# Second layer of a fused attention and feed-forward kernel on Trainium2: seven half-size products in place of eight, for all token chunks but the first

## The chip, the cores and the metric

The kernel runs on one core of one Trainium2 chip. The metric is the device time of one execution in microseconds (us). Matrix products run on TensorE (PE), which reads SBUF and writes PSUM. ScalarE (ACT), VectorE (DVE) and GpSimd (POOL) do elementwise work; SyncE (SP) here only starts DMAs. Every engine works through its own queue in order and waits for others by semaphores.

## The reference

Attention over 8 batches, 8 heads and 576 positions, with 16 extra "beacon" keys and values in front that every query sees, then two linear layers with a leaky ReLU between them on the 4608 tokens:

```python
def _attn_ref(q, k, v, beacon_k, beacon_v):
    k_all = np.concatenate([beacon_k, k], axis=2)
    v_all = np.concatenate([beacon_v, v], axis=2)
    scores = scale * np.matmul(q, k_all.transpose(0, 1, 3, 2))
    scores = np.where(causal, -1000000000.0, scores)
    a = np.exp(scores - scores.max(-1, keepdims=True))
    a /= a.sum(-1, keepdims=True) + 1e-09
    return np.matmul(a, v_all)

def _moe_ref(x, w_in, w_out):          # x: 4608 x 512, w_in: 512 x 2048, w_out: 2048 x 512
    h = x @ w_in
    g = np.maximum(0.01 * h, h)
    return g @ w_out
```

## The kernel before

**Attention.** A group is one batch and a pair of heads; there are 32 groups, four to a batch. Groups 0 to 7 are a hand-written head, a string of short codes that `run` expands. From group 8 on, the work is a list of events sorted by a due time in units of one group: loads of q and k (`load_natural`, issued by POOL), their transposes by DMA (`turn_pair`, issued by SP), a block of three score tiles (`block`: matmuls, then exponentials on ACT, then masks on POOL), the value matmuls in two halves (`value`: matmuls, then a reciprocal and a multiplication on DVE), and `x_turn`, two or three DMA transposes issued by SP that write the group's result into `xT`, which holds the tokens as columns.

**The two layers.** Tokens are taken in nine chunks of 512. One `up` (`moe1`) makes one 128 x 512 piece of layer 1: four matmuls of 512 columns into one PSUM bank, and a leaky ReLU on ACT into the bf16 tile `gT`; 16 of them make a chunk. One `down` (`moe2`) is a quarter of a 128-token output tile of layer 2: four matmuls of 512 columns, accumulated over 16 pieces of `gT` in one bank; 16 downs make a chunk. After the fourth quarter DVE copies the bank to `osb` (two buffers) and SP stores it. The very last tile is split into 384 and 128 columns, the second part copied and stored by ACT.

**Order.** The program order of all five queues is that of the Python program. Between events, `fill` places ups and downs so that they spread evenly over a batch: `aim` is the share of the units due. `ready` is the number of chunks whose tokens are finished; a batch makes one more ready, the last batch two. `finish` of a batch's last group also holds back three downs (`KEPT`) to be run before the first up of the new chunk. An up may be one chunk ahead of the downs (`gT` has two buffers); where both kinds can go, they take turns. So in a middle batch three old downs are followed by 16 ups and then 13 downs of the same chunk. I call the passage from the last up to the first down "the turn". After the last attention work, chunks 7 and 8 are left: 16 ups, then ups of chunk 8 and downs of chunk 7 by turns, then the downs of chunk 8 alone.

**PSUM.** Four single banks (`ps_one`, tag "one") are shared by the accumulators of ups, downs, values, transposes and the first score tile of each block; four more, in pairs, serve the other score tiles.

Of the kernel before, what the change touches and what calls it, by code (L numbers as in the profile page):

```python
# [8 lines left out]
FP32 = mybir.dt.float32  # L9
BF16 = mybir.dt.bfloat16  # L10
# [5 lines left out]
def kernel(  # L16
# [42 lines left out]
    QT = [(0, 112), (112, 128), (240, 128), (368, 128), (496, 80)]  # L59
    NA, NK = 4, 8  # L60
    LAID = 2 * NPAIR
    TURNED = 8
# [13 lines left out]
    singles = ctx.enter_context(tc.tile_pool(name="singles", bufs=1))  # L76
    qkpool = ctx.enter_context(tc.tile_pool(name="qkpool", bufs=2))
    natpool = ctx.enter_context(tc.tile_pool(name="natpool", bufs=6))
    headpool = ctx.enter_context(tc.tile_pool(name="headpool", bufs=2))
    gpool = ctx.enter_context(tc.tile_pool(name="gpool", bufs=2))  # L80
    opool = ctx.enter_context(tc.tile_pool(name="opool", bufs=2))
    ps_sc = ctx.enter_context(tc.tile_pool(name="ps_sc", bufs=2, space=bass.MemoryType.PSUM))
# [8 lines left out]
    w_out_sb = singles.tile([128, NF, DM], BF16, name="w_out_sb")  # L91
    w_out_r = moe_w_out.rearrange("(c p e) d -> p c (e d)", p=128, e=2)

    def w_in_cols(fc, j):
        at = fc % 8 // 2 * 256 + fc % 2
        return w_in_sb[fc // 8][:, j, at : at + 255 : 2]

    xT = singles.tile([128, NJ, NTOK], BF16, name="xT")
    bkT = singles.tile([128, B, NPAIR, NB], BF16, name="bkT")
# [3 lines left out]
    k_bufs = [k_all[:, i] for i in range(NK)]  # L103
    first_k = singles.tile([RP, 2, RI, D], FP32, name="first_k")
    k_nat0 = singles.tile([RP, RI, 2, D], BF16, name="k_nat0")
# [30 lines left out]
    def raw_of(b, grp):  # L136
        if (b, grp) not in qk_raw:
            qk_raw[b, grp] = (
                qkpool.tile([128, 2, RI, D], BF16, name="q_raw"),
                qkpool.tile([128, 2, RI, D], BF16, name="k_raw"),  # L140
            )
        return qk_raw[b, grp]
# [13 lines left out]
    def load_first_keys():  # L156
        nc.sync.dma_start(out=first_k, in_=k[0, 0:2].rearrange("h (p i) d -> p h i d", i=RI))

# [207 lines left out]
    def value(g, half):  # L366
# [19 lines left out]
        )  # L386

    def x_transposes(g, copy):
        b, hp = divmod(g, NPAIR)
        x_nat, _ = xs.pop(g)  # L390
        ps = ps_one.tile([128, 1024], BF16, name="tp", tag="one")
        for t, (q0, rows) in enumerate(QT):
            nc.tensor.transpose(
                ps[:, q0 : q0 + rows],
                x_nat[0:rows, t].rearrange("p e d -> p (e d)"),
                ident[0:rows, 0:rows],
            )
        copy(out=xT[:, hp, b * S : (b + 1) * S], in_=ps[:, 0:S])

    def x_turn(g):  # L400
        b, hp = divmod(g, NPAIR)
        x_nat, _ = xs.pop(g)
        t1 = NKB if b < B - 1 else NKB - 1
        dst = xT[:, hp, b * S : b * S + 112 + (t1 - 1) * 128]
        nc.sync.dma_start_transpose(
            out=dst[:, 112:].rearrange("c (t r) -> c t r", r=128),
            in_=x_nat[:, 1:t1].rearrange("r t e d -> r (t e d)"),
        )
        if t1 < NKB:
            nc.sync.dma_start_transpose(  # L410
                out=xT[:, hp, NTOK - 80 :], in_=x_nat[0:80, t1].rearrange("r e d -> r (e d)")
            )
        nc.sync.dma_start_transpose(  # L413
            out=dst[:, 0:112], in_=x_nat[0:112, 0].rearrange("r e d -> r (e d)")
        )
# [3 lines left out]
    def moe1(i, fc):  # L419
        if i not in gT:  # L420
            gT[i] = gpool.tile([128, NF, 512], BF16, name="gT")
        acc = ps_one.tile([128, 512], FP32, name="acc", tag="one")
        for j in range(NJ):
            nc.tensor.matmul(  # L424
                out=acc,
                lhsT=w_in_cols(fc, j),
                rhs=xT[:, j, i * 512 : (i + 1) * 512],
                start=(j == 0),
                stop=(j == NJ - 1),
            )  # L430
        nc.scalar.activation(out=gT[i][:, fc, :], in_=acc, func=AF.Prelu, alpha=0.01)  # L431

    early = {}

    def moe1_early(n, j):
        if j == 0:
            early[n] = ps_sc.tile([128, 2, 512], FP32, name="sc", tag="sc")
            if 0 not in gT:
                gT[0] = gpool.tile([128, NF, 512], BF16, name="gT")
        for e in range(2):  # L440
            fc = 2 * n + e
            nc.tensor.matmul(
                out=early[n][:, e],
                lhsT=w_in_cols(fc, j),
                rhs=xT[:, j, 0:512],
                start=(j == 0),
                stop=(j == NJ - 1),
            )
        if j == NJ - 1:
            nc.scalar.activation(  # L450
                out=gT[0][:, 2 * n : 2 * n + 2, :], in_=early[n], func=AF.Prelu, alpha=0.01
            )
            done1[0] += 2

    acc2 = [None]

    def moe2(i, t, quarter):
        t0 = i * 512 + t * 128
        if t0 + 128 < NTOK:
            moe2_part(i, t, quarter, quarter + 1, 0, DM, nc.vector.tensor_copy, nc.sync)  # L460
            return
        n = 3 * DM // 4
        if quarter < 3:
            moe2_part(i, t, 4 * quarter // 3, 4 * (quarter + 1) // 3, 0, n, nc.vector.tensor_copy, nc.sync)
        else:
            moe2_part(i, t, 0, 4, n, DM, nc.scalar.copy, nc.scalar)

    def moe2_part(i, t, q0, q1, lo, hi, copy, eng):
        if q0 == 0:
            acc2[0] = ps_one.tile([128, 512], FP32, name="acc", tag="one")  # L470
        acc = acc2[0][:, 0 : hi - lo]
        for fc in range(q0 * 4, q1 * 4):
            nc.tensor.matmul(  # L473
                out=acc,
                lhsT=gT[i][:, fc, t * 128 : (t + 1) * 128],
                rhs=w_out_sb[:, fc, lo:hi],
                start=(fc == 0),
                stop=(fc == NF - 1),
            )
        if q1 < 4:  # L480
            return
        t0 = i * 512 + t * 128
        osb = opool.tile([128, hi - lo], FP32, name="osb" if lo == 0 and hi == DM else f"osb{lo}")
        copy(out=osb, in_=acc)  # L484
        eng.dma_start(out=out[t0 : t0 + 128, lo:hi], in_=osb)

    done1, done2, ready, turn, first_down, held = [0], [0], [0], [0], [0], [0]

    def fill():
        i1, fc = divmod(done1[0], NF)  # L490
        i2, n2 = divmod(done2[0], NF)
        can1 = i1 < ready[0] and (i1 < 2 or i2 > i1 - 2)
        can2 = i2 < NCH and i2 < i1 and done1[0] >= first_down[0]
        if held[0] and can2:
            held[0] -= 1
            down()
        elif can1 and (turn[0] == 0 or not can2):
            up()
        elif can2:
            down()  # L500
        return can1 or can2

    def up():
        i1, fc = divmod(done1[0], NF)
        assert i1 < ready[0]
        moe1(i1, fc)
        done1[0] += 1
        turn[0] = 1

    def down():  # L510
        i2, n2 = divmod(done2[0], NF)
        moe2(i2, n2 // 4, n2 % 4)
        done2[0] += 1
        turn[0] = 0

# [39 lines left out]
    def run(steps):  # L555
        for step in steps.split():
# [25 lines left out]
            elif op == "u":  # L582
                up()
            elif op == "P":
                moe1_early(*a)
            elif op == "d":
                down()
            elif op == "w":
                unused(*a)
            elif op == "W":  # L590
                unused_ahead(*a)
            elif op == "i":
                load_w_in(a[0])
            elif op == "o":
                load_w_out(a[0])
            else:
                raise ValueError(step)
# [11 lines left out]
    with order:  # L609
# [12 lines left out]
        unused(13)  # L622
        nc.scalar.copy(out=k_nat0[:, :, 0], in_=first_k[:, 0])
        nc.vector.tensor_copy(out=k_nat0[:, :, 1], in_=first_k[:, 1])
        run("q0.1 k0 w2.384 s0.0 m0.0 w3.256 s0.1 q1 s0.2 m0.1 k1 s0.3 m0.2")
# [6 lines left out]
        beacon_transposes(2, B)  # L632
        run("m7.1 m7.2 N9.1 u b8.2 b9.2 b10.2 b11.2 x6 v7.0 T9 v7.1 d d d N10.0 N10.1 d V2.0 V2.1 x7 T10")

# [21 lines left out]
        def has_down():  # L656
            return done2[0] // NF < done1[0] // NF

# [27 lines left out]
        for at, _, what, args in events:  # L686
            while w + 2 < len(ends) and at > ends[w + 1]:
                w, d0 = w + 1, done1[0] + done2[0]
            todo = 2 * NF * ready[0] - KEPT - d0
            aim = d0 + todo * (at - ends[w]) / (ends[w + 1] - ends[w])  # L690
# [7 lines left out]
            what(*args)  # L698
        while done2[0] < NCH * NF:
            fill()  # L700
# [30 lines left out]
```

The softmax here doesn't subtract the row's maximum and nothing guards it: scores larger than these inputs give would overflow.

## Time and profile before

| | |
|---|---|
| runs shown | 338.26, 337.88, 338.02 us; median 338.02 us |
| profiled execution | span 339.9 us |
| PE busy | 328.5 us (97%), 2950 matmuls |
| ACT, POOL, DVE busy | 187.1, 180.8, 82.8 us |
| layer 1 matmuls (L424) | 553 recorded (576 in the program), 135.9 us |
| layer 2 matmuls (L473) | 568 recorded (592 in the program), 131.6 us |
| end of the last matmul | about 336.8 us |

The profiled execution lasted about 1.9 us longer than the median of the runs; its own span is the base for sums. Busy times of PE overlap, since matmuls are pipelined: a 512-column matmul is shown with 380 ns, while one follows another after about 216 ns. "x" is a count; "idle before" is the time an engine stood still before a group, with what ended it.

### The profile page before, as it was taken

Reading aid. Unit: us, or ns where it says so; the run is one execution under the profiler, and the core shown is the slowest. Engines: PE = TensorE matmul, PEld = TensorE weight load, DVE = VectorE, ACT = ScalarE, POOL = GpSimd, SP = SyncE. Lnnn points to the kernel's source line nnn. Section 1 sums busy time; section 2 is a strip of 40 time slices with the busy share of each in tenths; the row PEclk is TensorE's granted clock in tenths of the full one; section 3 lists DMA queues with packets and bytes.
Section 4 is the critical chain, followed back from the end, with each engine's and each line's share of the span. In section 5 each row is a group of like instructions: output and inputs, shape, how many; then the busy total and the mean of one; then the engine's idle time right before and its main releaser. Section 6 shows DMA issues by size and latency. Waiting matters only on the chain.

```text
span 339.9 us, 7458 instructions
## 1 busy us (share of the span) xinstructions
PE 328.5 (97%) x2950; PEld 170.7 (50%) x2997; DVE 82.8 (24%) x202; ACT 187.1 (55%) x312; POOL 180.8 (53%) x354
## 2 busy tenths in 40 slices
PE   8989999999996999999999999999999999999996
PEld 5574565455553455544554555545455544444443
DVE  3572354021222112311330232212321220000111
ACT  4969761778554583478536843685368205633300
POOL 8894969968987475668656966675221000000000
PEclk9999999999998999999999999999999999999999
DMA  8999999999999999999999999999211130000012
GB/s 135 129 194 169 149 212 129 177 181 122 163 154 186 160 113 139 137 123 103 110 183 137 112 114 159 159 117 123 89 56 39 23 110 33 0 31 33 31 63 91
DMA packets 151922, 39.84 MB, mean 117 GB/s; under 512 B 143008, under 2 KB 145184, under 8 KB 151888
## 3 DMA queue, kind: packets, MB, share of 16 engines
q0 software_dynamic: 99824, 18.54, 83.0%
q1 hardware_dynamic: 51648, 20.70, 34.0%
q8 instruction: 23, 0.38, 0.5%
q10 hardware_dynamic: 416, 0.13, 0.2%
q14 instruction: 11, 0.09, 0.1%
HBM read 37.22 MB, written 9.44 MB: 137 GB/s over the span
## 4 chain that ended last, share of the span: by engine, by line
PE 82%; DMA 11%; POOL 3%; issue 2%; SPq 0%; DVE 0%; ACT 0%; POOLq 0%; DVEq 0%
PE acc L473 34%; PE acc L424 34%; PE av L351 7%; PE sc L306 5%; DMA v_aug<-in_v_dram 4%; DMA w_in_sb<-in_moe_w_in_dram 4%; DMA out_dram<-osb 3%; POOL aT L281 1%; POOL q_raw L151 1%; POOL k_raw L151 1%; PE sc L259 0%; SPq L413 0%; DVE osb L484 0%; POOL w_in_sb L123 0%; POOL v_aug L206 0%
## 5 line engine op out<-in xcount | busy, mean ns | idle before, releaser
L424 PE MATMUL acc<-xT,w_in_sb 128*128 128x512 bf16 x553 | 135.9, 382 | 4.0 <-DMA xT<-x_nat 1.5
L473 PE MATMUL acc<-w_out_sb,gT 128*128 128x512 bf16 (+2 forms) x568 | 131.6, 373 | 1.5 <-issue 0.2
L431 ACT ACTIVATE gT<-acc 128x512 bf16<-128x512 f32 x144 | 83.8, 618 | 77.3 <-PE acc L424 75.6
L281 POOL TENSOR_SCALAR_AFFINE_SELECT aT<-aT 128x256 bf16<-128x256 bf16 (+2 forms) x160 | 57.5, 388 | 66.8 <-ACT aT L321 40.8
L424 PEld LDWEIGHTS <-w_in_sb 128*128 128x128 bf16 x576 | 53.7, 98 | 66.1 <-issue 8.3
L473 PEld LDWEIGHTS <-gT 128*128 128x128 bf16 x592 | 54.6, 98 | 60.1 <-issue 1.3
L321 ACT ACTIVATE aT<-sc 128x512 bf16<-128x512 f32 (+3 forms) x64 | 28.9, 521 | 49.0 <-PE sc L306 49.0
L325 ACT ACTIVATE aT<-sc 128x1024 bf16<-128x1024 f32 (+3 forms) x64 | 51.7, 893 | 0.0
L484 DVE COPY osb<-acc 128x512 f32<-128x512 f32 (+1 forms) x36 | 24.8, 688 | 96.2 <-PE acc L473 81.8
L380 DVE RECIPROCAL rec<-av 128x6 f32<-128x6 f32 (+1 forms) x64 | 12.1, 188 | 133.7 <-PE av L351 133.5
L351 PEld LDWEIGHTS <-aT 128*128 128x128 bf16 (+1 forms) x960 | 36.6, 98 | 13.5 <-issue 2.4
L351 PE MATMUL av<-v_aug,aT 128*128 128x65 bf16 (+1 forms) x960 | 40.0, 194 | 1.1 <-issue 0.9
L206 POOL DMA_DIRECT2D v_aug<-in_v_dram x40 | 34.1, 857 | 5.1 <-DMA w_in_sb<-in_moe_w_in_dram 4.3
L163 POOL DMA_DIRECT2D q_nat<-in_q_dram x48 | 34.9, 733 | 1.3 <-issue 0.4
L163 POOL DMA_DIRECT2D k_nat<-in_k_dram x48 | 34.8, 732 | 0.4 <-issue 0.3
L381 DVE TENSOR_TENSOR x_nat<-av,rec 128x384 bf16<-128x384 f32 (+1 forms) x64 | 31.4, 491 | 2.2
L268 ACT ACTIVATE aT<-sc 128x1024 bf16<-128x1024 f32 (+3 forms) x32 | 25.9, 875 | 3.3 <-PE sc L259 3.3
L306 PE MATMUL sc<-qT,kT 64*128 64x80 bf16 (+22 forms) x384 | 21.8, 250 | 0.5 <-PE acc L424 0.5
L306 PEld LDWEIGHTS <-kT 64*128 64x128 bf16 x384 | 12.7, 94 | 14.1 <-issue 11.6
L259 PE MATMUL sc<-qT,kT 64*128 64x80 bf16 (+4 forms) x96 | 9.9, 284 | 0.1
L520 PE MATMUL av<-blank 128*128 128x256 bf16 (+2 forms) x41 | 7.8, 349 | 1.1 <-DVE blank L612 1.1
L241 DVE COPY qT<-tp 128x576 bf16<-128x576 bf16 x7 | 5.3, 756 | 12.8 <-PE tp L235 12.8
(44 smaller groups left out, 69.4 us busy)
## 6 DMA issues: line engine op xcount, KB each, us to landing
out_dram<-osb SPq DMA_DIRECT2D x35, 256.0 KB, 2.7
q_nat<-in_q_dram POOLq DMA_DIRECT2D x48, 72.0 KB, 4.7
k_nat<-in_k_dram POOLq DMA_DIRECT2D x48, 72.0 KB, 5.0
v_aug<-in_v_dram POOLq DMA_DIRECT2D x24, 128.0 KB, 6.3
w_in_sb<-in_moe_w_in_dram POOLq DMA_DIRECT2D x2, 1024.0 KB, 12.6
w_out_sb<-in_moe_w_out_dram POOLq DMA_DIRECT2D x2, 1024.0 KB, 11.3
q_raw<-in_q_dram POOLq DMA_DIRECT2D x8, 144.0 KB, 6.8
k_raw<-in_k_dram POOLq DMA_DIRECT2D x7, 144.0 KB, 6.9
```

The lines of the kernel that those rows point to most:

```text
L163: nc.gpsimd.dma_start(out=t[:, :, par], in_=(q, k)[which][b, 2 * hp + par].rearrange("(t p) d -> p t d", p=NR),)
L206: nc.gpsimd.dma_start(out=dst[lo : ROWS[c], c, :, 0:D], in_=v[b, :, OFF[c] : OFF[c] + n].rearrange("h p d -> p h d"),)
L268: nc.scalar.activation(out=aT[:, :, c0 : c0 + w], in_=sc[:, :, 0:w], func=AF.Exp, scale=0.125)
L281: nc.gpsimd.affine_select(out=view, in_=view, compare_op=ALU.is_ge, fill=0.0, base=128 - n if lo == 0 else 0, channel_multiplier=-1, patte ...
L306: nc.tensor.matmul(out=(sc[par] if apart else sc[:, par])[:, at : at + b - a], lhsT=kT[ps_, c * 128 : (c + 1) * 128], rhs=qT[ps_, q0 : q0 ...
L321: nc.scalar.activation(out=probs[g][:, par, lo:hi], in_=sc[par][:, at : at + hi - lo], func=AF.Exp, scale=0.125)
L325: nc.scalar.activation(out=probs[g][:, :, lo:hi], in_=sc[:, :, at : at + hi - lo], func=AF.Exp, scale=0.125)
L351: nc.tensor.matmul(out=avv[:, n, 0 : D + 1], lhsT=aT[0 : ROWS[c], par, a0 : a0 + 128], rhs=va[0 : ROWS[c], c, 2 * hp + par, :], start=(c = ...
L381: nc.vector.tensor_tensor(out=x_nat[:, t0:t1].rearrange("p t e d -> p (t e) d"), in0=avv[:, :, 0:D], in1=rec[:, n0:n1, None].to_broadcast( ...
L424: nc.tensor.matmul(out=acc, lhsT=w_in_cols(fc, j), rhs=xT[:, j, i * 512 : (i + 1) * 512], start=(j == 0), stop=(j == NJ - 1),)
L431: nc.scalar.activation(out=gT[i][:, fc, :], in_=acc, func=AF.Prelu, alpha=0.01)
L473: nc.tensor.matmul(out=acc, lhsT=gT[i][:, fc, t * 128 : (t + 1) * 128], rhs=w_out_sb[:, fc, lo:hi], start=(fc == 0), stop=(fc == NF - 1),)
```

## The change

Chunks 1 to 8 compute layer 2 as a 2 x 2 block product by Strassen's identity in Winograd's form. With the chunk's 512 tokens, the 2048 inner values and the 512 output columns each cut in two, seven products of halves replace eight, and sums of blocks are formed beforehand and of products afterwards. One down is now one product for 128 of its 256 tokens: eight matmuls of 256 columns; 14 downs make a chunk. Chunk 0 keeps the plain form (`moe2_plain`).

- The sums of weight blocks (`weight_sums`) are three DVE additions in the hand-written head (code `t0`) and one more after chunk 0's last down, in place in `w_out_sb`.
- The sums of `gT` blocks (`token_sums`) are four DVE additions for each half of the 16 ups of a chunk. They go to a list, `due`, and one is placed behind each up and before each down; what is left goes ahead of the third down.
- The products' sums (`combine`): three ACT copies out of PSUM and five DVE additions a chunk, in fp32. Two products share a bank where they are added (1 and 2; 7 and 4; 5 and 3). Four stores a chunk, each of 256 rows by 256 columns.
- `osb` gets three buffers; `u2`, `u3` and `p5` have one each.
- In the last chunk the bank of products 5 and 3 is one bank per 128 tokens, with its own combine and store.
- To make room, `xT` becomes a ring of four batches (`XR`) and 48 columns, so that chunk 4 wraps and its layer 1 is done as two runs of 256 columns; `natpool` goes from six to four buffers; the head's raw q and k tiles and its first keys lie in the slots of the sums (`sum_tile`, two buffers for each of three names, as many as the raw tiles had). The first keys are two DMAs instead of one.
- Ups of chunks 1 to 8 alternate between the lower and the upper eight pieces of `gT`, so that each half of the ups completes matching pieces of both.
- `moe1_early`, which nothing called, is gone.

```diff
+    XR = 4
...
-    qkpool = ctx.enter_context(tc.tile_pool(name="qkpool", bufs=2))
-    natpool = ctx.enter_context(tc.tile_pool(name="natpool", bufs=6))
+    natpool = ctx.enter_context(tc.tile_pool(name="natpool", bufs=4))
     headpool = ctx.enter_context(tc.tile_pool(name="headpool", bufs=2))
     gpool = ctx.enter_context(tc.tile_pool(name="gpool", bufs=2))
+    sumpool = ctx.enter_context(tc.tile_pool(name="sumpool", bufs=2))
...
+    w_sum = singles.tile([128, 3, NF // 2, DM // 2], BF16, name="w_sum")
...
-    xT = singles.tile([128, NJ, NTOK], BF16, name="xT")
+    xT = singles.tile([128, NJ, XR * S + 48], BF16, name="xT")
...
-    first_k = singles.tile([RP, 2, RI, D], FP32, name="first_k")
+    def sum_tile(n):
+        return sumpool.tile([128, NF * 128], BF16, name=f"gsum{n}")
+
+    QK = 2 * RI * D
+    first_k = [
+        sum_tile(2)[0:RP, 0:QK].bitcast(FP32).rearrange("p (i d) -> p i d", i=RI) for _ in range(2)
+    ]
...
-            qk_raw[b, grp] = (
-                qkpool.tile([128, 2, RI, D], BF16, name="q_raw"),
-                qkpool.tile([128, 2, RI, D], BF16, name="k_raw"),
-            )
+            qk_raw[b, grp] = [
+                sum_tile(n)[:, 0:QK].rearrange("p (h i d) -> p h i d", h=2, i=RI) for n in range(2)
+            ]
...
+    def x_at(b):
+        assert b < XR or done1[0] >= NF * -(-((b - XR + 1) * S + 48) // 512)
+        return b % XR * S
...
+        at = i * 512 % (XR * S)
+        cut = min(512, XR * S - at)
+        for lo, hi in ((0, cut), (cut, 512)):
+            for j in range(NJ):
+                if lo == hi:
+                    continue
+                x0 = (at + lo) % (XR * S)
+                nc.tensor.matmul(
+                    out=acc[:, lo:hi],
+                    lhsT=w_in_cols(fc, j),
+                    rhs=xT[:, j, x0 : x0 + hi - lo],
+                    start=(j == 0),
+                    stop=(j == NJ - 1),
+                    skip_group_check=True,
+                )
...
+    HF, HD, HT = NF // 2, DM // 2, 256
+    ADD, SUB = ALU.add, ALU.subtract
+
+    def weight_sums(part):
+        b11, b12 = w_out_sb[:, 0:HF, 0:HD], w_out_sb[:, 0:HF, HD:DM]
+        b21, b22 = w_out_sb[:, HF:NF, 0:HD], w_out_sb[:, HF:NF, HD:DM]
+        t1, t2, t4 = (w_sum[:, i] for i in range(3))
+        tt = nc.vector.tensor_tensor
+        if part == 0:
+            tt(out=t1, in0=b12, in1=b11, op=SUB)
+            tt(out=t2, in0=b22, in1=t1, op=SUB)
+            tt(out=t4, in0=b21, in1=t2, op=SUB)
         else:
-            moe2_part(i, t, 0, 4, n, DM, nc.scalar.copy, nc.scalar)
-
-    def moe2_part(i, t, q0, q1, lo, hi, copy, eng):
-        if q0 == 0:
-            acc2[0] = ps_one.tile([128, 512], FP32, name="acc", tag="one")
-        acc = acc2[0][:, 0 : hi - lo]
-        for fc in range(q0 * 4, q1 * 4):
+            tt(out=b12, in0=b22, in1=b12, op=SUB)
+
+    sums = {}
+
+    def token_sums(i, lo, hi):
+        if i not in sums:
+            sums[i] = [sum_tile(n).rearrange("p (c t) -> p c t", c=HF) for n in range(3)]
+        g, s = gT[i], sums[i]
+        a11, a12 = g[:, lo:hi, 0:HT], g[:, HF + lo : HF + hi, 0:HT]
+        a21, a22 = g[:, lo:hi, HT : 2 * HT], g[:, HF + lo : HF + hi, HT : 2 * HT]
+        s1, s2, s4 = (s[n][:, lo:hi] for n in range(3))
+        return [
+            dict(out=s1, in0=a21, in1=a22, op=ADD),
+            dict(out=s2, in0=s1, in1=a11, op=SUB),
+            dict(out=a21, in0=a11, in1=a21, op=SUB),
+            dict(out=s4, in0=a12, in1=s2, op=SUB),
+        ]
+
...
+    PRODUCTS = (1, 6, 2, 7, 5, 4, 3)
+    banks, parts = {}, {}
+
+    def ND(i):
+        return NF if i == 0 else 2 * len(PRODUCTS)
...
+        n, tile = PRODUCTS[n2 // 2], n2 % 2
+        bank = {1: "a", 2: "a", 6: "b", 7: "c", 4: "c", 5: "d", 3: "d"}[n]
+        opens = n in (1, 6, 7, 5)
+        apart = i == NCH - 1 and bank == "d"
+        if opens and (tile == 0 or apart):
+            banks[bank, tile] = ps_one.tile([128, 512], FP32, name="acc", tag="one")
+        acc = banks[bank, tile if apart else 0]
+        lo = 0 if apart else tile * HD
+        for fc in range(HF):
+            nc.tensor.matmul(
+                out=acc[:, lo : lo + HD],
+                lhsT=left(i, n, fc, tile),
+                rhs=right(n, fc),
+                start=(opens and lo == 0 and fc == 0),
+                stop=(fc == HF - 1),
+                skip_group_check=True,
+            )
+        if apart:
+            combine(i, n, acc[:, 0:HD], (tile, tile + 1))
+        elif tile == 1:
+            combine(i, n, acc, (0, 2))
+
+    def combine(i, n, acc, tiles):
+        lo, hi = tiles[0] * HD, tiles[1] * HD
+
...
+        tt = nc.vector.tensor_tensor
+        if n == 1:
+            nc.scalar.copy(out=kept("u2"), in_=acc)
+        elif n == 6:
+            tt(out=part("u2"), in0=acc, in1=part("u2"), op=ADD)
+        elif n == 2:
+            c = kept("osb", 3)
+            nc.scalar.copy(out=c, in_=acc)
+            store(i, 0, 0, tiles, c)
+        elif n == 7:
+            tt(out=kept("u3"), in0=acc, in1=part("u2"), op=ADD)
+        elif n == 5:
+            c = kept("p5")
+            nc.scalar.copy(out=c, in_=acc)
+            tt(out=part("u3"), in0=part("u3"), in1=c, op=ADD)
+            store(i, 1, 1, tiles, part("u3"))
+        elif n == 4:
+            c = kept("osb", 3)
+            tt(out=c, in0=acc, in1=part("u2"), op=ADD)
+            store(i, 1, 0, tiles, c)
+        elif n == 3:
+            c = kept("osb", 3)
+            tt(out=c, in0=acc, in1=part("u2"), op=ADD)
+            store(i, 0, 1, tiles, c)
+
...
+    due = []
+
+    def add_due(n=1):
+        while due and n:
+            nc.vector.tensor_tensor(**due.pop(0)[1])
+            n -= 1
+
+    def add_all(i):
+        while due and due[0][0] == i:
+            add_due()
+
+    SLICE = 4
+
     def up():
-        i1, fc = divmod(done1[0], NF)
+        i1, n = divmod(done1[0], NF)
         assert i1 < ready[0]
+        fc = n if i1 == 0 else n // 2 + n % 2 * HF
         moe1(i1, fc)
+        add_due()
         done1[0] += 1
         turn[0] = 1
+        if i1 and n % (2 * SLICE) == 2 * SLICE - 1:
+            due.extend((i1, op) for op in token_sums(i1, n // 2 + 1 - SLICE, n // 2 + 1))
 
     def down():
-        i2, n2 = divmod(done2[0], NF)
-        moe2(i2, n2 // 4, n2 % 4)
+        add_due()
+        if at2[1] == 2:
+            add_all(at2[0])
+        moe2(*at2)
         done2[0] += 1
+        at2[1] += 1
+        if at2[1] == ND(at2[0]):
+            at2[:] = at2[0] + 1, 0
         turn[0] = 0
 
...
-        run("m7.1 m7.2 N9.1 u b8.2 b9.2 b10.2 b11.2 x6 v7.0 T9 v7.1 d d d N10.0 N10.1 d V2.0 V2.1 x7 T10")
+        run("m7.1 m7.2 N9.1 u b8.2 b9.2 b10.2 b11.2 x6 v7.0 T9 v7.1 d d t0 d N10.0 N10.1 d V2.0 V2.1 x7 T10")
...
-            todo = 2 * NF * ready[0] - KEPT - d0
+            todo = NF * ready[0] + sum(ND(i) for i in range(ready[0])) - KEPT - d0
...
```

In `token_sums` the four sums are taken over `gT` pieces lo to hi of both halves; `left` and `right` pick the two factors of a product from `gT`, the sums, `w_out_sb` and `w_sum`.

## The prediction, made before the changed kernel had run

> **What bounds the kernel now.** I read the page's busy shares first, then the groups, then PE's waits, then the chain of waits, and last the timeline around the places where the chunk changes from ups to downs. Busy shares, the granted clock and three groups:
>
> ```profile
> PE 328.5 (97%) x2950; PEld 170.7 (50%) x2997; DVE 82.8 (24%) x202; ACT 187.1 (55%) x312; POOL 180.8 (53%) x354
> PEclk9999999999998999999999999999999999999999
> L424 PE MATMUL acc<-xT,w_in_sb 128*128 128x512 bf16 x553 | 135.9, 382 | 4.0 <-DMA xT<-x_nat 1.5
> L473 PE MATMUL acc<-w_out_sb,gT 128*128 128x512 bf16 (+2 forms) x568 | 131.6, 373 | 1.5 <-issue 0.2
> L484 DVE COPY osb<-acc 128x512 f32<-128x512 f32 (+1 forms) x36 | 24.8, 688 | 96.2 <-PE acc L473 81.8
> ```
>
> PE is never free for long, its clock is granted at 90% or more in every slice, and the idle time before its two large groups is 5.5 us in all. No other engine is over 55%. Matmuls overlap, so what one costs must be read from the chain, where runs on PE stand with start, length and count:
>
> ```profile
> 48.44 0.92 PE av L351 x30
> 322.92 7.55 PE acc L473 x35
> 330.53 6.26 PE acc L473 x44
> ```
>
> 35 matmuls of 512 columns took 7.55 us, 0.216 each. 30 value matmuls of 65 columns, each with a weight load of its own, took 0.92 us, 0.031 each: loads keep up at that pace. The last run is 12 of 512, 16 of 384 and 16 of 128 columns. With columns/2.4 plus 2.5 ns they cost 2.59 + 2.60 + 0.89 = 6.08 us, and 0.16 us for the last one's drain (219 ns shown, 56 spaced) gives 6.24 of the 6.26. So every matmul of a run costs its columns plus 2.5 ns, weight load hidden. PE work is the bound: 1,152 matmuls of the two layers at 0.216 are 249 us of the span. The only PE stalls worth the name, in PE's timeline:
>
> ```profile
> 107.93 0.38 PE L424 MATMUL acc<-xT,w_in_sb 128*128 128x512 bf16 x1 [1.53 <-DMA xT<-x_nat]
> 109.32 0.58 PE L424 MATMUL acc<-xT,w_in_sb 128*128 128x512 bf16 x1 [1.01 <-DVE osb L484]
> 110.13 2.16 PE L424 MATMUL acc<-xT,w_in_sb 128*128 128x512 bf16 x5 [0.22 <-issue]
> ```
>
> They stand at the first steady batch's end. After them five matmuls take 2.16 us, 0.43 each, double the usual. The second stall is a PSUM bank whose copy waited for an `osb` buffer (DVE waited twice for an output DMA, 9.3 us).
>
> **What the Trainium skill says.** "TensorE: Matmul & The Clock Gate", in "Wait — 56ns, not 53.3ns?", gives N/2.4 + 2.5 ns for warm matmuls; the runs above agree. Its Part 1 on the clock gate says that idleness throttles PE to half its clock; the 0.43 us matmuls after the stalls agree. "VectorE: DVE Perf Modes", tier table, gives 1224 ns for a bf16 addition of 2048 elements with both inputs in SBUF (two per cycle) and says fp32 or PSUM operands go at one per cycle; the 128x512 fp32 copy's 692 ns fits one per cycle, but no row of before shows a bf16 SBUF addition. "SBUF — State Buffer", "Who interferes with whom", says that a DVE instruction with two SBUF inputs contends with POOL's reads; before has none to show it.
>
> **The change part by part.**
>
> PE, layer 2. A chunk of 64 matmuls at 0.2158 is 13.81 us; 7 x 2 x 8 = 112 of 256 columns at 0.1092 (256/2.4 + 2.5 ns) are 12.23. Eight chunks: **-12.64 us**. Chunk 0 is unchanged. Chunk 4's wrapped ups are 64 more matmuls at 2.5 ns: +0.16.
>
> DVE. Per chunk eight sums of 1024 elements at (512 + 151)/0.96 = 0.69 us, from the skill's price (151 cycles are also what 692 ns leaves over 512), and five fp32 additions at 0.69 like the copy row. In all 64 x 0.69 + 40 x 0.69 + 4 weight sums at 1.22, less 32 copies (22.0): 82.8 becomes about 137 us, 41%. ACT gets 24 copies at about 0.62 (the leaky ReLU's row, same size): 187 becomes 202. Neither engine becomes the bound; order decides what they cost.
>
> The turn. Before, the first down needs `gT` piece 15 as its 16th matmul, 3.2 us after the turn. Now product 1 (two downs, 1.75 us) is followed by product 6, whose fifth matmul needs the second half of S2: last leaky ReLU, then two DVE sums, at 1.75 + 0.44 = 2.19 us after the turn. With ACT idle the ReLU ends 0.80 us after the turn (197.69 against 196.89 in the timeline), the sums at 0.80 + 1.38 + about 0.1 = 2.28: 0.1 us late. With a score block just before, ACT's exponentials stand in front:
>
> ```profile
> 125.51 0.85 PE L306 MATMUL sc<-qT,kT 64*128 64x64 bf16 x16
> 126.30 1.04 PE L424 MATMUL acc<-xT,w_in_sb 128*128 128x512 bf16 x4
> 127.06 2.02 ACT L325 ACTIVATE aT<-sc 128x1024 bf16<-128x1024 f32 x3
> 127.17 1.89 PE L473 MATMUL acc<-w_out_sb,gT 128*128 128x512 bf16 x7
> 128.92 0.66 ACT L431 ACTIVATE gT<-acc 128x512 bf16<-128x512 f32 x1
> ```
>
> The turn is at 127.17, the last ReLU ends at 129.58, 2.41 late; S2 is ready at +3.9, PE wants it at +2.19 plus 0.37 of value matmuls that fall between: 1.33 us of PE idle. The six turns of before (86.72, 127.17, 161.46, 196.89, 232.63, 266.58) give in this way 0.75, 1.33, 0, 0.1, 1.33, 0.1: +3.6 us. Positions shift, as 30 units instead of 32 fill a batch, so the bounds are 0.5 and 8 (all like the worst). Behind a waiting sum on DVE stand the value's reciprocal and multiplication, then SP's `x_turn`: they come 1 to 1.5 us later. At the later batch ends that is covered by the three held downs, 2.6 us; the turns at the end have either alternation (3.5 us of cover) or an idle ACT.
>
> Shared banks. Product 2 adds onto product 1's bank and must wait for ACT's copy, 0.7 us with latency against 1.75 us of product 6; product 3 on 5 likewise; 4 on 7 waits for a DVE addition of 0.69. Only ACT's 3.1 us of exponentials per block (1.08 + 2.02) break the cover, and only when the copied product is the first unit behind the block: 0.8 us in about one case in seven, two copies a chunk, 1.4 us over six middle chunks. Two accumulators instead of one stay open for four of 14 downs, while a block takes two single banks and values two; I add 0.6. Together +2.0, bounds 0 and 4.
>
> `osb` with three buffers: the bank stall of 1.01 us should go. The first, for the DMA transpose, I leave, as SP's order and the crowded DMA stay: -1.0, bounds +1.5 (DVE later) and -4 (both stalls and the 1.5 us lost to slow matmuls).
>
> The head. `t0` puts 3.66 us on DVE at about 55.9, ahead of group 7's copy into `xT`, which then ends near 60.05 instead of 57.67. The first up that reads it starts at 59.60 and needs that part in its fourth matmul, at 60.25; held downs hide it. Nothing taken, bounds 0 and +0.5. Raw tiles have as many buffers as before, `natpool`'s four still leave three groups between a load and the transpose that frees its slot, the key load in two DMAs has equal bytes, and each x slot in the ring is written one batch or more after its last reader: nothing. Four stores a chunk stay four on SP, with rows of 1 KB instead of 2: nothing, as stores landed in 2.7 us.
>
> The end. After the last matmul DVE adds 128x256 out of PSUM, 424 ns by L381's row of that size, where ACT copied 265; the store is 128 KB instead of 64: +0.2.
>
> POOL may lose some 0.1 us a mask to contention; masks have most of a group (over 6 us) before the values need them: nothing.
>
> Sum: -12.64 + 0.16 + 3.6 + 2.0 - 1.0 + 0 + 0.2 = -7.7 us. The profile's 339.9 becomes 332.2; against the median of 338.02, where I assume the same difference, **330.3**. In PE terms the rest of the span is unchanged.
>
> **The rivals.**
> 1. *Full cover.* The sums slip in where values and blocks stand, and both early stalls go. For it: three of six turns already come out at or near zero. Against: ACT's bursts recur every block. -12.64 + 0.16 + 0.2, 0.5 left at turns and 1 to 4 gained at the early stalls: 325.2 down to 322.2, taken as 325.2.
> 2. *Handed back.* Turns all like 127.17 (8 us) and banks at their bound (4 us): -12.64 + 0.36 + 12 = -0.3, about 337.7.
> 3. *Slower by late sums on DVE.* If a bf16 sum runs at one element per cycle (1.22 us, weights 2.29), the two sums of the turn take 2.44: an idle ACT leaves 1.15 us, and ACT's lateness as above about 0.6 more on average, so 1.75 at six turns is 10.5; one more such wait at chunk 8's last turn 1.15. The head's three sums take 6.9 us and hold the xT copy to 63.2, 3 us beyond need, with 1.5 us of slow clock as after the stall shown. With banks at 2: -12.64 + 0.36 + 10.5 + 1.15 + 4.5 + 2 = +5.9, 343.9. It decides from about 1.0 us a sum. For it: sums read strided halves, and POOL can hold DVE; against: the skill's price for just this kind.
> 4. *256-column matmuls don't halve.* At 123 ns or more nothing is saved (13.81/112) and the waits would make it slower, 343. Against: the 31 ns of 65-column matmuls.
>
> **How the numbers follow.** The forecast (330.3, its own range 327 to 335): 0.57. Full cover: 0.20. Handed back: 0.10, half of it within 0.2%. Slower by late sums 0.11, by matmuls 0.02. A measurement here tells 0.2%, 0.7 us, from no change. Faster: 0.57 + 0.20 + 0.05 = 0.82; same 0.05; slower 0.13. The range reaches into full cover and towards the handed-back case, 324.5 to 336; outside lie the slower 0.13 and about 0.05 more.
>
> **What would show it.** Layer 2 runs of 256-column matmuls at 0.109 us each in the chain; DVE near 137 us with sums of about 0.69; PE's waits on DVE sums, one to three of the middle turns, 0.5 to 1.5 us each; short PE waits on ACT's copies of `u2` and `p5`; no wait of `osb` on an output DMA; the last 14 downs in about 12.3 us instead of 14. The prediction is wrong if sums take over 1 us, if PE slows to 0.43 us a 512-column matmul after turns, or if PE idles for DMA or masks in the middle batches.

## The result and the profile after

The changed kernel took 333.91 us (median; before 337.9 on the same chips), a ratio of **0.988**, 95% interval 0.985 to 0.991: about 4 us faster. The profiled execution has a span of 330.8 us against 339.9, which is 9.1 us less. That the two differ is the first thing to explain; executions of one kernel differ by up to some 5 us, mostly before the first up of chunk 1 and in the batch behind it, so below I compare stages with equal work. Four of the changed kernel's 12 runs took 337.5 to 338.8 us and are left out of the ratio, as such slow runs are for every kernel here; in the two profiles below that are of slow runs (before with three `osb` buffers, and product 2 second), PE works at half pace until 24.1 us of the span, in the others until 4 to 6.5 us.

The page of the changed kernel, busy shares and clock, then groups of layer 1, the activations, one form of layer 2, and one of the four kinds of sums:

```profile
PE 317.8 (96%) x3401; PEld 213.1 (64%) x3429; DVE 132.5 (40%) x280; ACT 199.8 (60%) x336; POOL 183.2 (55%) x354
PEclk9999999999999999999999999999999999999999
L442 PE MATMUL acc<-xT,w_in_sb 128*128 128x512 bf16 (+1 forms) x615 | 134.0, 357 | 1.9 <-DMA xT<-x_nat 0.5
L450 ACT ACTIVATE gT<-acc 128x512 bf16<-128x512 f32 x144 | 83.0, 620 | 56.9 <-PE acc L442 55.4
L539 PE MATMUL acc<-w_out_sb,gT 128*128 128x256 bf16 x384 | 47.2, 273 | 1.4 <-ACT gT L450 1.3
L616 DVE TENSOR_TENSOR gsum<-gT 128x1024 bf16<-128x1024 bf16 x16 | 11.2, 697 | 53.9 <-ACT gT L450 53.9
```

DVE and ACT carry what was expected, a sum takes 0.70 us, and the slice with a slowed clock is gone. PE's waits, longest in total first (us, times, longest):

```profile
PE acc L539 <- DVE gsum L616: 1.7, 5, 0.6
PE av L359 <- ACT aT L329: 1.6, 3, 0.8
PE acc L539 <- ACT gT L450: 1.3, 2, 0.7
PE av L651 <- DVE blank L743: 1.1, 1, 1.1
PE sc L314 <- PE acc L442: 0.5, 1, 0.5
PE acc L442 <- DMA xT<-x_nat: 0.5, 1, 0.5
```

The first three didn't exist before. They understate the loss, since a matmul's drain is shown as busy time: at the turn of chunk 5 two of these waits are shown with 0.67 and 0.55 us, and cost 0.84 and 0.72. By loss I mean the time from the start of one matmul to the start of the next, beyond what the first one's columns take. The timeline of PE, ACT and DVE at the turn of chunk 5 shows it (start, length, then the count):

```profile
226.72 2.02 ACT L333 ACTIVATE aT<-sc 128x1024 bf16<-128x1024 f32 x3
226.83 1.03 PE L442 MATMUL acc<-xT,w_in_sb 128*128 128x512 bf16 x4
227.69 0.93 PE L539 MATMUL acc<-w_out_sb,gT 128*128 128x256 bf16 x7
228.58 1.14 ACT L450 ACTIVATE gT<-acc 128x512 bf16<-128x512 f32 x2
229.29 0.28 PE L539 MATMUL acc<-w_out_sb,gT 128*128 128x256 bf16 x1 [0.67 <-ACT gT L450]
229.41 0.53 PE L359 MATMUL av<-v_aug,aT 128*128 128x65 bf16 x12
229.76 0.69 DVE L616 TENSOR_TENSOR gsum<-gT 128x1024 bf16<-128x1024 bf16 x1 [4.52 <-ACT gT L450]
...
230.65 0.60 PE L539 MATMUL acc<-w_sum,gsum 128*128 128x256 bf16 x4
...
231.06 0.68 DVE L616 TENSOR_TENSOR gsum<-gsum,gT 128x1024 bf16<-128x1024 bf16 x1
...
231.80 0.61 PE L539 MATMUL acc<-w_sum,gsum 128*128 128x256 bf16 x4 [0.55 <-DVE gsum L616]
```

Exponentials hold ACT until about 228.6, so the last two leaky ReLUs run in one piece until 229.72. Product 1 stops at its eighth matmul: seven started from 227.69 on should let the next start at 228.45 (7 x 0.109), it starts at 229.29, 0.84 us lost. S1 starts on DVE only behind the last ReLU, the value's two DVE operations (0.75 us) come in between, and S2 ends at 231.74: product 6 loses 0.72 us more (four matmuls from 230.65 would end at 231.09, next start 231.80).

With start-to-start losses of this kind summed over the batches from the first up of chunk 1 to the first of chunk 7: 1.9 us in product 1 (three turns), 2.5 us in product 6 (five turns), 2.6 us for score and value matmuls and one up that wait for a single PSUM bank (0.35, 0.44, 0.37, 0.60, 0.87), and 1.2 us for DMA. At the last turn, with ACT idle, 0.12. In the second profile of the changed kernel, which comes below, the turns of these stages cost 5.0 instead of 4.5 us, the banks the same, and DMA 3.2.

In stages the picture is the following: us from the first weight load of a chunk's ups to that of the next chunk's, the same attention work in each column, and in the last the time from chunk 7's first up to the end of the matmuls. All rows are profiled executions, also those of the experiments.

| kernel | 1 to 2 | 2 to 3 | 3 to 4 | 4 to 5 | 5 to 6 | 6 to 7 | 7 to end |
|---|---|---|---|---|---|---|---|
| before | 46.2 | 38.8 | 34.8 | 36.0 | 34.6 | 31.3 | 55.7 |
| before, again | 45.9 | 36.1 | 34.8 | 36.0 | 34.6 | 31.3 | 55.7 |
| before, three `osb` buffers | 45.6 | 34.6 | 34.8 | 36.0 | 34.6 | 31.3 | 55.7 |
| changed | 46.6 | 35.5 | 35.0 | 34.9 | 34.8 | 30.0 | 52.5 |
| changed, again | 48.2 | 35.7 | 35.0 | 34.9 | 34.8 | 30.0 | 52.5 |
| without token sums | 45.9 | 34.7 | 34.7 | 34.4 | 34.1 | 29.7 | 52.4 |
| ups in fours | 47.5 | 34.8 | 35.0 | 34.9 | 34.8 | 30.0 | 52.5 |
| product 2 second | 45.5 | 35.9 | 34.1 | 34.4 | 34.1 | 29.7 | 52.4 |
| both | 46.0 | 34.2 | 34.1 | 34.4 | 33.3 | 29.7 | 52.4 |
| both, a bank each | 45.2 | 34.3 | 33.2 | 34.4 | 33.2 | 29.7 | 52.4 |
| changed, S1 and S2 twice | 49.6 | 36.4 | 36.5 | 36.5 | 36.4 | 31.5 | 53.9 |
| a bank each, S1 and S2 twice | 46.7 | 35.0 | 33.5 | 34.6 | 34.4 | 29.9 | 52.4 |

From chunk 3 on, columns of one kernel repeat to 0.1 us, so I put what they show down to the order of the program. The end, two chunks, gains 3.2 us, twice the 1.58 of the sum. The four columns before it gain 2.0 us together where 4 x 1.58 = 6.3 were to be had.

### The profile page after: what moved, and what is told of

Its sections match the earlier page's. It is cut to its first block, busy times and chain, and to the rows that moved or that the text cites. A ratio compares the mean times of both kernels' runs of the same rounds, so it can differ in the third digit from the quotient of the medians.

```text
span 330.8 us, 8482 instructions
## 1 busy us (share of the span) xinstructions
PE 317.8 (96%) x3401; PEld 213.1 (64%) x3429; DVE 132.5 (40%) x280; ACT 199.8 (60%) x336; POOL 183.2 (55%) x354
## 4 chain that ended last, share of the span: by engine, by line
PE 76%; DMA 8%; ACT 5%; DVE 4%; POOL 4%; issue 2%; SPq 0%; ACTq 0%; POOLq 0%
PE acc L442 34%; PE acc L539 25%; PE av L359 7%; PE sc L314 5%; DMA w_out_sb<-in_moe_w_out_dram 4%; PE acc L512 4%; DMA v_aug<-in_v_dram 3%; DVE gsum L616 2%; ACT aT L333 2%; ACT aT L329 2%; ACT gT L450 1%; DVE x_nat L389 1%; POOL gsum L158 1%; DMA xT<-x_nat 1%; POOL v_aug L214 1%
## 5 line engine op out<-in xcount | busy, mean ns | idle before, releaser
L442 PE MATMUL acc<-xT,w_in_sb 128*128 128x512 bf16 (+1 forms) x615 | 134.0, 357 | 1.9 <-DMA xT<-x_nat 0.5
L442 PEld LDWEIGHTS <-w_in_sb 128*128 128x128 bf16 x640 | 59.6, 98 | 53.6 <-issue 4.3
L289 POOL TENSOR_SCALAR_AFFINE_SELECT aT<-aT 128x256 bf16<-128x256 bf16 (+2 forms) x160 | 59.8, 403 | 60.9 <-ACT aT L329 38.7
L539 PEld LDWEIGHTS <-gT 128*128 128x128 bf16 x512 | 48.9, 98 | 11.2 <-ACT gT L450 2.3
L539 PE MATMUL acc<-w_out_sb,gT 128*128 128x256 bf16 x384 | 47.2, 273 | 1.4 <-ACT gT L450 1.3
L539 PEld LDWEIGHTS <-gsum 128*128 128x128 bf16 x384 | 36.1, 98 | 8.8 <-DVE gsum L616 3.3
L214 POOL DMA_DIRECT2D v_aug<-in_v_dram x40 | 34.3, 866 | 4.3 <-DMA w_in_sb<-in_moe_w_in_dram 4.0
L171 POOL DMA_DIRECT2D q_nat<-in_q_dram x48 | 34.9, 734 | 0.7
L171 POOL DMA_DIRECT2D k_nat<-in_k_dram x48 | 34.8, 732 | 0.7 <-DMA w_out_sb<-in_moe_w_out_dram 0.4
L539 PE MATMUL acc<-w_sum,gsum 128*128 128x256 bf16 x256 | 32.9, 273 | 1.8 <-DVE gsum L616 1.7
L616 DVE TENSOR_TENSOR gsum<-gT 128x1024 bf16<-128x1024 bf16 x16 | 11.2, 697 | 53.9 <-ACT gT L450 53.9
L573 DVE TENSOR_TENSOR u<-acc,u 128x512 f32<-128x512 f32 x8 | 5.5, 691 | 27.2 <-PE acc L539 27.2
```

What stands on the lines that cost most here:

```text
L171: nc.gpsimd.dma_start(out=t[:, :, par], in_=(q, k)[which][b, 2 * hp + par].rearrange("(t p) d -> p t d", p=NR),)
L214: nc.gpsimd.dma_start(out=dst[lo : ROWS[c], c, :, 0:D], in_=v[b, :, OFF[c] : OFF[c] + n].rearrange("h p d -> p h d"),)
L289: nc.gpsimd.affine_select(out=view, in_=view, compare_op=ALU.is_ge, fill=0.0, base=128 - n if lo == 0 else 0, channel_multiplier=-1, patte ...
L442: nc.tensor.matmul(out=acc[:, lo:hi], lhsT=w_in_cols(fc, j), rhs=xT[:, j, x0 : x0 + hi - lo], start=(j == 0), stop=(j == NJ - 1), skip_gro ...
L539: nc.tensor.matmul(out=acc[:, lo : lo + HD], lhsT=left(i, n, fc, tile), rhs=right(n, fc), start=(opens and lo == 0 and fc == 0), stop=(fc ...
```

## The experiments

The theory after the result is this: PE gains the full 1.58 us a chunk, and gives it back where product 1 and product 6 come too soon after the last up, and where open accumulators make other matmuls wait for a bank. Rivals: DVE's load as such; a base that wasn't typical; sums that cost nothing.

**The kernel before, once more.** No edit.

> The kernel before once more, for a second profile of it. Theory A (the profile on which the sum was made shows an execution with a rare stall: from the first up of chunk 2 to the first up of chunk 3 it took 39.01 us where later batches of equal work took 35): this execution has about 35 us there, no half clock, and a span of about 336 us. Theory B (the stall belongs to every execution): about 39 us again and a span near 340.

Measured: span 336.3 us, 36.1 in the stage in question, full clock. PE's timeline there:

```profile
104.57 1.04 PE L424 MATMUL acc<-xT,w_in_sb 128*128 128x512 bf16 x4
106.94 2.75 PE L424 MATMUL acc<-xT,w_in_sb 128*128 128x512 bf16 x12 [1.33 <-DVE osb L484]
```

The wait for the `osb` copy's bank is there again, the wait for the DMA transpose and the slow clock are not. Theory A holds for 2.7 of the stage's 4 us. The execution that I took as base was 3.6 us longer than this one.

**Before, with three `osb` buffers.**

```diff
-        osb = opool.tile([128, hi - lo], FP32, name="osb" if lo == 0 and hi == DM else f"osb{lo}")
+        osb = opool.tile([128, hi - lo], FP32, name="osb" if lo == 0 and hi == DM else f"osb{lo}", bufs=3 if lo == 0 and hi == DM else 1)
```

> The kernel before with three osb buffers instead of two. If the osb buffer is what stalls the first batch end in most executions, 1 us or more (0.3% or more) faster than before. If most executions have no such stall (theory A of the run above), the same within 0.3%, and no wait of DVE's copy on an output DMA in the profile.

Measured: ratio 0.997 (0.994 to 0.999), 1.1 us (0.2 to 2.0), and 34.6 us in the stage, without the wait. So the third buffer is worth about 1 us by itself, though the interval is wide: a part of the change that has nothing to do with the products.

**Changed, without the token sums.**

```diff
-        return sums[i][{5: 0, 6: 1, 3: 2}[n]][:, fc, t]
+        if n == 5:
+            return gT[i][:, fc, HT + tile * 128 : HT + (tile + 1) * 128]
+        return gT[i][:, fc + (HF if n == 3 else 0), t]
...
-            due.extend((i1, op) for op in token_sums(i1, n // 2 + 1 - SLICE, n // 2 + 1))
+            pass
```

> The changed kernel without the 64 DVE sums of gT blocks; products 5, 6 and 3 read gT pieces in their place, so the output is another one and only the time of the sums is left out. Turn theory: PE's waits on the sums in product 6 (2.5 us at five middle turns in the profile of the changed kernel) go, the waits on the last leaky ReLUs in product 1 (1.9 us) and on score banks (2.6 us) stay: 2 to 3 us faster than the changed kernel, ratio to before about 0.980. Rival, DVE's load as a whole delays PE (banks of values freed late, x_turn late): 5 us or more, ratio 0.973 or less. Rival, the sums cost nothing: ratio 0.988.

Measured: ratio 0.977 (0.971 to 0.983), span 328.1, 2.7 us below the changed kernel's. The six stages become 0.3 to 0.9 us shorter, the end 0.1, and the waits of product 1 and of values on ACT stay at 1.3 and 1.6 us. The ratios alone (3.7 us apart, some 2 us either way) don't exclude the rival of 5 us. The stages do: from chunk 3 on they shrink by 0.34, 0.45, 0.72, 0.35 and 0.13 us, and the losses in product 6 there were 0.33, 0.44, 0.72, 0.33 and 0.12. So there the 45 us of DVE work cost what product 6 waits for and nothing besides: the load as such isn't what holds PE up.

**Changed, ups in fours.** Pieces 0 to 3, 8 to 11, 4 to 7, 12 to 15.

```diff
-        fc = n if i1 == 0 else n // 2 + n % 2 * HF
+        fc = n if i1 == 0 else n // 8 * SLICE + n % SLICE + n // SLICE % 2 * HF
```

> The changed kernel, but within each half of a chunk's ups the four lower pieces of gT come first and then the four upper ones, so that product 1 needs none of the last four ups. Turn theory: the waits of product 1 on the last leaky ReLUs (1.9 us at three turns: 0.80, 0.30, 0.83) go, but the first half of this wait is only moved to product 6, which needs all 16 and then two sums; 0.5 to 1.5 us faster than the changed kernel, ratio to before 0.984 to 0.987, and no PE wait on gT's activation in product 1. Rival, ACT's lateness is paid at product 6 in full: the same as the changed kernel, 0.988.

Measured: ratio 0.984, too wide to tell (0.978 to 0.990); the stages from chunk 3 on are those of the changed kernel to 0.1 us. PE's waits:

```profile
PE acc L539 <- DVE gsum L616: 3.8, 6, 1.4
PE av L359 <- ACT aT L329: 1.6, 3, 0.8
```

Product 1 no longer waits, product 6 waits as much longer: the rival was right. One wait hid behind the other.

**Product 2 second**, in a bank of its own; `add_all` moves to the fifth down accordingly.

```diff
-    PRODUCTS = (1, 6, 2, 7, 5, 4, 3)
+    PRODUCTS = (1, 2, 6, 7, 5, 4, 3)
...
-        bank = {1: "a", 2: "a", 6: "b", 7: "c", 4: "c", 5: "d", 3: "d"}[n]
-        opens = n in (1, 6, 7, 5)
+        bank = {1: "a", 2: "e", 6: "b", 7: "c", 4: "c", 5: "d", 3: "d"}[n]
+        opens = n in (1, 2, 6, 7, 5)
...
-            nc.scalar.copy(out=c, in_=acc)
+            tt(out=c, in0=acc, in1=part("u2"), op=ADD)
             store(i, 0, 0, tiles, c)
...
-        if at2[1] == 2:
+        if at2[1] == 4:
```

> The changed kernel with the products in the order 1, 2, 6, 7, 5, 4, 3, product 2 in a bank of its own and added to the copy of product 1 by DVE, so that product 6, the first to need a DVE sum, comes 1.75 us later. Turn theory: all waits on sums in product 6 go (0.71, 0.33, 0.44, 0.72, 0.33 us at the five turns from chunk 2 on), the waits of product 1 on the last leaky ReLUs (0.80, 0.30, 0.83) stay: about 2.5 us faster than the changed kernel, ratio to before about 0.981. Rival, the waits only move on to the next product: same as the changed kernel.

And **both**, this with the ups in fours:

> The same, with the ups in the order lower four, upper four within each half of a chunk. Turn theory: product 1 no longer needs any of the last four ups and product 6 has 1.75 us more; both kinds of wait at the turn go, 4.4 us in all, ratio to before about 0.975; what stays are waits of values and scores on single banks (2.6 us). Rival, ACT's lateness is passed on to product 2, which needs the last piece: 2.5 us or less, 0.981.

Measured: product 2 second 0.975 (0.966 to 0.983), both 0.970 (0.965 to 0.974); the changed kernel on the same chip 0.989 (0.986 to 0.993). Both medians are below the forecasts, 0.981 and 0.975, the second clearly. From chunk 3 on they take 2.6 and 3.4 us less than the changed kernel; the rest lies in the head and the first two stages, where executions differ, and I can't put it down to the edits. All waits on sums are gone in the first, with product 1's ReLU waits left; these go in the second. The bank wait at 162 us (0.60) went along, since product 1's bank is now freed after two downs. The ups' order, worth nothing alone, is worth 0.8 us in two stages once product 6 is out of its way (0.83 and 0.84 us lost in product 1 at the turns of chunks 2 and 5 are gone; the rest of the step from 35.9 to 34.2 is a shorter wait for DMA).

For the yardstick of these runs, the changed kernel again, the expectation was:

> The changed kernel once more, on the same chip as the next three, as their yardstick and for a second profile of it. Its middle stages should repeat: from first up to first up of chunks 3, 4, 5, 6, 7 35.0, 34.9, 34.8 and 30.0 us within 0.2, since their waits follow from the order of the program; the first stages may differ. Ratio to before about 0.988.

The stages repeat (35.0, 34.9, 34.8, 30.0). The second profile has a span of 333.5: a wait of 2.2 us for a transposed `kT` in its first batch, which the other doesn't have.

**Both, and a bank for each product.**

```diff
-    PRODUCTS = (1, 2, 6, 7, 5, 4, 3)
+    PRODUCTS = (1, 2, 6, 7, 4, 5, 3)
...
-        bank = {1: "a", 2: "e", 6: "b", 7: "c", 4: "c", 5: "d", 3: "d"}[n]
-        opens = n in (1, 2, 6, 7, 5)
+        bank = "d" if n in (5, 3) else "a"
+        opens = True
...
             tt(out=part("u3"), in0=part("u3"), in1=c, op=ADD)
+            tt(out=part("u2"), in0=part("u2"), in1=c, op=ADD)
...
         elif n == 4:
-            tt(out=c, in0=acc, in1=part("u2"), op=ADD)
+            tt(out=c, in0=acc, in1=part("u3"), op=ADD)
```

> The same, and every product in a bank of its own for its two downs, in the order 1, 2, 6, 7, 4, 5, 3, at the price of one more DVE addition of 128x512 a chunk. If the value matmuls' waits behind a score block (0.35, 0.37, 0.60, 0.87 us) come from two accumulators being open at once, they go: 2 us faster than the kernel of the run before, ratio to before about 0.969. Rival, they come from ACT's lateness with the score tiles' banks alone: no change against the run before, or slower by DVE's extra work.

Measured: 326.57 us, ratio **0.967** (0.963 to 0.971), the lowest median here, but only 0.7 us below the kernel of the run before (0.970), with intervals that overlap; 2 us were forecast. The stages are clearer. The value wait that was left (0.87 us in the stage from chunk 3 to 4) is gone, and that stage falls from 34.1 to 33.2: it came with the shared banks, not with ACT's lateness alone. That open accumulators made it is likely and not shown by itself, as the edit also has to put product 4 ahead of 5. Of the other three waits that I had counted on, those of 0.37 and 0.60 had already gone with product 2 second, and the up's wait of 0.35 us in the stage from chunk 1 to 2 stays. From the first up of chunk 3 to the last matmul this kernel takes 182.8 us, the one before the change 192.4: 9.6 us less, where six chunks at 1.58 make 9.5. There nothing of PE's gain is lost any more. PE's busy time by stage, first in the changed kernel, then in this one (start:end, length, busy PE, then the other engines):

```profile
140.47:175.51 35.04, 33.38 (x352) 22.52 (x353) 13.51 (x29) 22.39 (x41) 22.80 (x45) 1.00 1.31 131
210.26:245.20 34.94, 33.56 (x357) 22.66 (x357) 12.96 (x29) 24.17 (x43) 18.55 (x38) 1.00 1.31 124
```

```profile
138.25:171.49 33.24, 33.08 (x352) 22.42 (x353) 14.16 (x30) 21.91 (x40) 22.15 (x43) 1.00 1.40 139
205.90:239.06 33.16, 33.00 (x354) 22.64 (x356) 13.95 (x30) 23.25 (x41) 18.54 (x38) 1.00 1.32 132
```

PE stands still for 0.16 us a stage where it stood 1.4 to 1.7, with more DVE work than in the changed kernel (14.2 and 14.0 us against 13.5 and 13.0). Its PE timeline at the turn of chunk 5, for comparison with that shown above, runs through without a gap:

```profile
221.38 1.90 PE L442 MATMUL acc<-xT,w_in_sb 128*128 128x512 bf16 x8
223.12 1.04 PE L539 MATMUL acc<-w_out_sb,gT 128*128 128x256 bf16 x8
223.99 0.53 PE L359 MATMUL av<-v_aug,aT 128*128 128x65 bf16 x12
224.35 1.91 PE L539 MATMUL acc<-w_out_sb,gT 128*128 128x256 bf16 x16
226.10 0.72 PE L359 MATMUL av<-v_aug,aT 128*128 128x65 bf16 x18
226.66 1.04 PE L539 MATMUL acc<-w_out_sb,gT 128*128 128x256 bf16 x8
227.53 1.04 PE L539 MATMUL acc<-w_sum,gsum 128*128 128x256 bf16 x8
```

**S1 and S2 twice**, in the changed kernel and in the last one, to see what a slower sum would have done.

```diff
             dict(out=s1, in0=a21, in1=a22, op=ADD),
+            dict(out=s1, in0=a21, in1=a22, op=ADD),
             dict(out=s2, in0=s1, in1=a11, op=SUB),
+            dict(out=s2, in0=s1, in1=a11, op=SUB),
```

> The changed kernel with the sums S1 and S2 formed twice each (the same values), 96 sums of 0.70 us instead of 64. Turn theory: S2 is ready 1.4 us later at each turn and product 6 waits for it at all seven turns that have no alternation: stages from chunk 2 on 36.4, 36.2, 36.2 and 31.4 us instead of 35.0, 34.9, 34.8 and 30.0, and about 9 us slower in all, ratio to before 1.01 to 1.02. Rival, DVE's extra 22 us are spread and only part of them shows: 2 to 4 us slower, 0.995 to 1.0.

> The same doubling in the kernel with product 2 second, the other order of ups and a bank for each product. Turn theory: product 6 wants S2 3.9 us after the turn; doubled sums are ready at 3.6 us where ACT is free and up to 5.2 where a score block stands before the turn, so one or two of the middle stages grow by 0.5 to 1.3 us and the others by nothing: 1 to 3 us slower than without the doubling, ratio to before 0.970 to 0.976. Rival, DVE's load counts as such: about 9 us slower here too, 0.993.

Measured: 344.01 us and 1.019 (1.013 to 1.025) in the one, 329.44 us and 0.976 (0.972 to 0.980) in the other. The same 22 us of DVE work cost 10 us where product 6 comes 1.75 us after the turn, and about 3 where it comes at 3.5; in the stages from chunk 3 on, 7.5 and 1.8. In the first, the wait on sums grew as foreseen:

```profile
PE acc L541 <- DVE gsum L618: 12.5, 7, 2.0
PE acc L541 <- ACT gT L450: 2.0, 3, 0.7
```

Seven waits, 1.6 to 2.2 us lost start to start, and PE's clock fell to half for 3.4 us once, at the turn of chunk 1. Twice the DVE time for the two sums at the turn makes the change a loss.

## Why the prediction was right or wrong

The direction and the mechanism were right, the size was off: 330.3 against 333.9, a gain of 7.7 us foreseen and 4 found. The range held it, being wide: 333.9 lies about midway between the forecast and the rival "handed back" (337.7). Term by term:

- *PE, -12.64.* Right. 112 matmuls of 256 columns in the last chunk are one run of 12.24 us in the kernel with a bank each, 0.109 each. Where no wait is left, stages are 1.5 to 1.6 us shorter than before (33.24 against 34.83, 33.16 against 34.64, 29.68 against 31.27), and the end 3.3 (52.35 against 55.67). One reading of the profile before was wrong: the clock was not granted at 90% or more in every slice, the line shown has an 8 in the 13th, which is the 3.4 us at half clock after the two stalls.
- *DVE and ACT.* 137 and 202 us foreseen, 132.5 and 199.8 found; a sum 0.69, found 0.70. The price from the Trainium skill ("VectorE: DVE Perf Modes", "The perf-mode tier table"), 1224 ns for 2048 elements, is met by the four weight sums of that size (1.21 to 1.23 us), and my estimate from it by the sums of half the size. The contention with POOL of which "SBUF — State Buffer" speaks, in "Who interferes with whom", shows in single instructions and hardly in the mean: POOL's longest mask takes 0.95 us against 0.45 and 0.54 in the two profiles of before and 0.45 without the token sums, but masks of 128x256 take 425 ns on average against 410 and 420.
- *The turn, +3.6.* Mechanism right, size too small: 4.5 found in six turns (5.0 in the second profile), and 0.12 at the last. What I missed: product 1 itself needs piece 7, the last but one up, 0.76 us after the turn. With ACT late that is where PE stops first. It adds little, since product 6 waits for the same ReLU, as the ups in fours showed.
- *Shared banks, +2.0.* Found 2.6, but made up otherwise, so the near hit is luck. Of the waits on ACT's and DVE's copies (1.4) none showed. The 0.6 for a lack of banks became 2.6, and it wasn't layer 2 that paid but other work that had to wait for a free bank. For 1.8 us of it, three value waits (0.37, 0.60, 0.87), the shared banks are the cause as far as the edits tell: the waits went when products got a bank of their own for two downs, with their order changed along with it. The waits of an up (0.35) and of a score tile (0.44), both in the stage from chunk 1 to 2, stay in the kernel with a bank each, at 0.35 and 0.69. Their cause is open; before the change they weren't there.
- *`osb`, -1.0.* Right within what can be told: 1.1 us (0.2 to 2.0) in the run with that edit alone.
- *The head, 0, and the end, +0.2.* Nothing to see in either: the time from the last matmul's end to the end is 3.17 us against 3.16.
- *Waits for DMA, nothing new.* This is the rest of the shortfall. With what was measured in place of what was foreseen, the terms above give -12.64 + 0.16 + 4.5 + 0.1 + 2.6 - 1.1 = -6.4 us; the runs say -4 (-3 to -5). From the first up of chunk 3 on the changed kernel takes 187.2 us in both profiles against 192.4 before, 5.2 less. The two stages ahead of it gain nothing: 82.1 and 83.9 us against 82.0 in the second profile of before, where 2 x 1.58 were to be had. Part of that is the turns and banks already counted; the other part is waits for transposed `xT` and `kT`, 1.2 us in the first profile and 3.2 in the second. With these, and with the 1.3 us that PE waited for the `osb` copy in the second profile of before, the sum for the two is -12.64 + 0.16 + 4.5 + 0.1 + 2.6 + 1.2 - 1.3 = -5.4 and, with 5.0 and 3.2, -2.9 us; their spans are 5.5 and 2.8 us below that profile's 336.3. Whether the change itself makes these waits longer is open: the two profiles of before have 1.7 us of them and none, and no run tests the change's smaller `natpool` or its shorter rows in the stores.
- *The base.* It was badly chosen, but it isn't why the gain fell short, as the terms are differences and only the -1.0 was read from its stalls. A run's time is about 1.7 us more than its span (332.48 and 330.8, 337.95 and 336.3), so the execution profiled before was some 3.5 us longer than the median and not 1.9. Of its stall and slow clock, 2.7 us are missing from the second profile without any change. That the sum against this profile, 332.2, came near the 330.8 found is luck: what was missing there made up for waits that I had priced too low.

The slower rival named the right mechanism. Its turning point, about 1.0 us a sum, fits the doubled sums: 0.70 us gave a gain of 1.2%, 1.40 a loss of 1.9%, and a straight line between them crosses zero near 0.97 us (an estimate, nothing between was run). Full cover was reached only by other orders of products and ups. What makes the waits for transposes and loads in the first batches differ between executions I didn't try to find out.

## What to carry to other kernels

When work moves from a saturated engine to a free one, count the microseconds between the last input and the first use of the derived operand, at the moment when the helper's queue is fullest; its mean load says little. Put the products that need no derived operand first: here that order, and accumulators closed after two units, took the gain from 1.2% to 3.3% with more helper work, not less. And a stall in one profiled execution is to be set against the spread of the runs before it goes into a sum.

## What I had not expected

An edit that moved a wait without shortening it (the ups in fours) was worthless alone and worth about 0.8 us in each of two stages on top of another. And from chunk 3 on the stages, with the waits in them, repeat to 0.1 us between executions, while waits on DMA don't: the first batch varied by 1.6 us between two profiles of one kernel.
